# Attention with mixture of depths on one core: first loads ahead of a branch, mixture layers spread evenly and begun earlier

## Chip, cores and metric

The kernel runs on one NeuronCore of a Trainium2 chip. The metric is device time in microseconds (us), the median of several runs. All arithmetic is in float32.

## The reference

There are 8 batches of 448 tokens and 12 heads of 64 dimensions. First comes attention with normalized queries and keys, then, for each batch, a gate picks 128 tokens that pass through a two-layer network:

```python
q_n, k_n = (rmsnorm(q, g_q), rmsnorm(k, g_k))
scores = scale * np.matmul(q_n, k_n.transpose(0, 1, 3, 2))
scores = scores - np.max(scores, axis=-1, keepdims=True)
attn = np.exp(scores)
attn = attn / (np.sum(attn, axis=-1, keepdims=True) + 1e-09)
x = np.matmul(attn, v)                      # then (B, H, S, D) -> (B, S, H*D)
scores = np.einsum('bsd,d->bs', x, w_gate)
for b in range(B):
    top_idx = np.argpartition(-scores[b], capacity)[:capacity]   # capacity = 128
    xe = x[b, top_idx]
    ye = np.maximum(xe @ w1, 0.0) @ w2                           # 768 -> 1024 -> 768
    g = 1.0 / (1.0 + np.exp(-scores[b, top_idx]))
    out[b, top_idx] = x[b, top_idx] + g[:, None] * ye
```

## The kernel before

**Branch.** The program first loads g_q and g_k on the queue of SP, bounds the scores from them on VectorE (the bound test, lines 1193 to 1198) and every engine branches on the outcome (L1205, L1207). The inputs take the branch `fast`; `general` is not executed.

**Groups and units.** Four heads make a group: three groups to a batch, 24 in all. Each group has seven units of 64 keys, 168 units in all. A unit is `scores` (PE, L278), the exponential of its scores on ScalarE (L287), `values` (PE, L304, accumulated over the seven units of a group) and the running sum of the exponentials on VectorE (L317). Ahead of that, a group's queries and keys are squared (ScalarE, L193), summed (VectorE, L199) and turned into reciprocal roots (GpSimd, L200 and L203). For groups 2 to 23 these go through memory (`rows_out`, `rows_in`) and scale the queries (`scale_q`); for groups 0 and 1 `scale_q_early` does it with matmuls (L249) and VectorE (L257).

**Start of `fast`.** SP issues the loads of groups 0 and 1 (L102) in the order tok(0,0), tok(0,1), q(0), tok(1,0), k(0), tok(1,1), v(0), q(1), k(1), v(1). ScalarE's queue loads the gain column gcol (L133) and loads its table with a first exponential (L139). VectorE makes `gg` from gcol (L145); this stands ahead of the first sum of squares in its program. PE runs 60 transposes of an identity (L151) before its first useful matmul.

**After a group.** `values_out` copies the two accumulators to xT. Then four tasks follow, one at a time: `sum_keys` (L339, copied at L350), `invert_sums` (L357, L359), and `to_tokens` for the two halves (L371, scaled on VectorE at L373). After the second half come `gate` (L397) and, for the third group of a batch, `store_x` (SP, L385) and `spread` (VectorE, L413). `ranks_of` is queued as the next task: `score_rows` (PE, L426, ScalarE L430), `count` (VectorE, L440), `annotate` (L459), `select` (four scatters on GpSimd into the memory tile `selected`, L467), and `load_selected` (SP, L485), which brings the selected tokens back as `xe`.

**The mixture layer of a batch** is a generator of ten pieces: two of transposes of `xe` (L505, copied by ScalarE at L510), four of the first matrix (L524, two of them to an activation at L533), four of the second (L543, two of them to a combination at L552). The last piece issues the scatter to the output on GpSimd (L561). The two of transposes are light on PE, the eight others (*heavy*) take some 2.7 us each.

**Order.** Everything is emitted by hand in program order, section by section; each engine runs its own part in that order. A section `q` has four units: first `scores` of its units with `values` behind them, then one task (`opening`), then two halves. In each half the work that was set for its slots is issued (`run`), then a mixture piece (`piece`), then one task. A slot is a unit's number, so section `q` holds slots 4q to 4q + 3. After section 41 the units are used up and the loop runs on until the layers are done. `ready[b]` is the first section in which the layer of batch b may begin:

```python
ready[b] = max((s + 4) // PER + 1, first_ff(b) - 1) if b < B - 1 else 0
```

Here `s` is the slot at which `ranks_of` ran, and `first_ff` is a lower bound that grows by 21 units with each batch. Once begun, a layer gives one piece to each half until it is done.

Of the kernel before, what the change touches and what calls it, by code (L numbers as in the profile page):

```python
# [23 lines left out]


@with_exitstack
def fast(
    ctx: ExitStack,
    tc: tile.TileContext,
    qT: bass.AP,  # L30
    kT: bass.AP,
    vp: bass.AP,
    tok: bass.AP,
    g2: bass.AP,
# [19 lines left out]

    B, NP, _, S = qT.shape
    CP = 112
# [16 lines left out]
    const = ctx.enter_context(tc.tile_pool(name="const", bufs=1))  # L73
    load_pool = ctx.enter_context(tc.tile_pool(name="load", bufs=2))
    norm_pool = ctx.enter_context(tc.tile_pool(name="norm", bufs=2))
# [21 lines left out]

    toks, qTs, kTs, vs, sss, rinvs, bcs = {}, {}, {}, {}, {}, {}, {}

    def load(name, store, src, shape, n, bufs):  # L100
        t = load_pool.tile(shape, F32, name=name, bufs=bufs)
        nc.sync.dma_start(out=t, in_=src)  # L102
        store[n] = t

    def load_tok(n, i):
        load("tok", toks, tok[n // NG, n % NG, :, i], [128, 2, NI, D], (n, i), 4)

    def load_q(n):
        c = n % NG * 2
        load("qT", qTs, qT[n // NG, c : c + 2].rearrange("c p s -> p c s"), [128, 2, S], n, 3)  # L110

    def load_k(n):
        c = n % NG * 2
        load("kT", kTs, kT[n // NG, c : c + 2].rearrange("c p s -> p c s"), [128, 2, S], n, 3)

    def load_v(n):
        load("v", vs, vp[n // NG, n % NG], [128, 2, NI, D], n, 3)

    ident = const.tile([128, 128], F32, name="ident")
    make_identity(nc, ident)  # L120
    load_tok(0, 0)
    load_tok(0, 1)
    load_q(0)
    load_tok(1, 0)
    load_k(0)
    load_tok(1, 1)
    load_v(0)
    load_q(1)
    load_k(1)
    load_v(1)  # L130

    gcol = const.tile([128, 2], F32, name="gcol")
    nc.scalar.dma_start(out=gcol, in_=g2)  # L133
    gg = const.tile([128, 1], F32, name="gg")
    neg_half = const.tile([128, 1], F32, name="neg_half")
    nc.vector.memset(neg_half, -0.5)

    warm = const.tile([128, 1], F32, name="warm")
    nc.scalar.activation(out=warm, in_=neg_half, func=AF.Exp)  # L139

# [8 lines left out]
    ps = ps_moe.tile([128, 512], F32, tag="moe", name="warm_ps")  # L149
    for _ in range(60):  # L150
        nc.tensor.transpose(out=ps[:, 0:128], in_=ident, identity=ident)  # L151
# [38 lines left out]
    def squares(n, i):  # L190
        t = toks.pop((n, i))
        sq = norm_pool.tile([128, 2, NI, D], F32, name="sq")
        nc.scalar.activation(out=sq, in_=t, func=AF.Square, scale=scale)  # L193
        sss[n, i] = norm_pool.tile([128, 2, NI], F32, name="ss", bufs=4)
        return sq
# [38 lines left out]
    def scale_q(n):  # L234

        t = qTs[n]
        nc.vector.scalar_tensor_tensor(
            out=t, in0=t, scalar=gg, in1=bcs.pop(n), op0=OP.mult, op1=OP.mult
        )

    def scale_q_early(n):

        rinv = rinvs.pop((n, 0))
        for c in range(2):
            ps = ps_sc.tile([128, 512], F32, tag="sc", name="sc")
            r = slice(D * c, D * (c + 1))
            for i in range(NI):
                for hh in range(2):
                    nc.tensor.matmul(  # L249
                        out=ps[D * hh : D * (hh + 1), D * i : D * (i + 1)],  # L250
                        lhsT=rinv[r, hh, i : i + 1].to_broadcast([D, D]),
                        rhs=ident[r, r],
                        start=True,
                        stop=True,
                    )
            t = qTs[n][:, c].rearrange("d (p i) -> d p i", i=NI)
            nc.vector.scalar_tensor_tensor(  # L257
                out=t,
                in0=t,
                scalar=gg,  # L260
                in1=ps[:, 0:S].rearrange("d (i p) -> d p i", i=NI),
                op0=OP.mult,
                op1=OP.mult,
            )
# [5 lines left out]
    def scores(u):  # L270
        n, i = divmod(u, NI)
        scs = [ps_sc.tile([128, 512], F32, tag="sc", name="sc") for _ in range(2)]
        for c in range(2):
            for k0 in (0, 32):
                for hh in range(2):
                    r = slice(D * hh, D * (hh + 1))
                    o = D * c + k0
                    nc.tensor.matmul(  # L278
                        out=scs[hh][o : o + 32, 0:S],
                        lhsT=kTs[n][r, c, D * i + k0 : D * i + k0 + 32],  # L280
                        rhs=qTs[n][r, c, :],
                        start=True,
                        stop=True,
                    )
        p = p_pool.tile([128, 2, S], F32, name="p")
        for hh in range(2):
            nc.scalar.activation(  # L287
                out=p[:, hh],
                in_=scs[hh][:, 0:S],
                func=AF.Exp,  # L290
                scale=rinvs[n, 1][:, hh, i : i + 1],
            )
        probs[u] = p

    def values(u):
# [3 lines left out]
        for hh in range(2):  # L299
            for d0 in (0, 32):  # L300
                for c in range(2):
# [3 lines left out]
                        out=avs[n][c][o : o + 32, 0:S],  # L305
                        lhsT=vs[n][r, hh, i, d0 : d0 + 32],
                        rhs=probs[u][r, hh],
# [266 lines left out]
    HALVES = 2  # L574
    PER = 2 * HALVES
    units = n_groups * NI
    todo, tasks = {}, []
# [25 lines left out]
    for n in range(1, n_groups):  # L603
        s0 = NI * n
        if n > 2:
            at(max(s0 - 26, 0), load_tok, n, 0)
            at(max(s0 - 26, 0), load_tok, n, 1)
        if n > 1:
            first = max(s0 - 18, 0)
            prepare(n, first)  # L610
            at(max(s0 - 7, first + 10), scale_q, n)
            at(max(s0 - 13, 2), load_q, n)
            at(max(s0 - 11, 2), load_k, n)
            at(max(s0 - 11, 2), load_v, n)
    for part in range(NDC + NFC):
# [21 lines left out]
    def last_tokens(n):  # L637
# [8 lines left out]
        q, place = now  # L646
        tasks.insert(0, ((q + 1, place // 2), lambda: ranks_of(b)))

    def ranks_of(b):
# [6 lines left out]
        at(s + 4 if s >= 0 else s + 3, load_selected, b)  # L656
        ready[b] = max((s + 4) // PER + 1, first_ff(b) - 1) if b < B - 1 else 0

    def first_ff(b):


        return -(-(units + 2 * PER - NG * NI * (B - 2 - b)) // PER)

# [20 lines left out]
    sum_squares(1, 1, sq.pop((1, 1)))  # L684
    load_tok(2, 0)
    load_tok(2, 1)
    tasks.append(((0, 1), lambda: scale_q_early(1)))
# [5 lines left out]

    def piece(q):

        nonlocal moe, done
        if next(moe, moe) is not moe:
            return True
        if ready.get(done, q + 1) > q:
            return False  # L700
        moe = mixture(done)
        done += 1
        next(moe)
        return True

    waiting = list(range(units))
    moe, ready, done, q = iter(()), {}, 0, 0
    while done < B or tasks:
        now[:] = q, 0
# [7 lines left out]
        for half in range(HALVES):  # L717
            run((k + 2 * half, k + 2 * half + 1))
            some = piece(q)
            spare[0] = not some and half == 0  # L720
# [4 lines left out]
        q += 1  # L725
    for _ in moe:
        pass


@with_exitstack  # L730
def general(
# [33 lines left out]
    load_pool = ctx.enter_context(tc.tile_pool(name="load", bufs=2))  # L765
    norm_pool = ctx.enter_context(tc.tile_pool(name="norm", bufs=2))
    tr_pool = ctx.enter_context(tc.tile_pool(name="tr", bufs=3))
# [12 lines left out]
    def load(n):  # L780

        b, h0 = n // NG, n % NG * GH
        for nm, src in (("q", q), ("k", k), ("v", v)):
            t = load_pool.tile(
                [CP, GH, NJ, D], F32, tag=nm, name=nm, bufs=5 if nm == "v" else 3
            )
# [186 lines left out]
    def mixture(b):  # L973
# [36 lines left out]
        for j in range(NJ):  # L1010
            cmp = moe_pool.tile([CP, S], F32, name="cmp", bufs=2)
            nc.vector.tensor_scalar(
# [7 lines left out]
            )  # L1020
            cmp = moe_pool.tile([CP, S], F32, name="cmp", bufs=2)
            nc.vector.scalar_tensor_tensor(
# [35 lines left out]
        for s in range(NSLOT):  # L1058
# [45 lines left out]
            for f0 in range(0, NFC, 4):  # L1104
                ps = bank()
                for i in range(4):
# [8 lines left out]
                    if i % 2:  # L1115
# [6 lines left out]
                        yield  # L1122
            y = moe_pool.tile([128, DM], F32, name="y", bufs=2)
            for half in range(2):
# [58 lines left out]
def _build(nc, ap, cap, out):  # L1183
    D = ap["g_q"].shape[0]
    with tile.TileContext(nc) as tc:
        with tc.tile_pool(name="bound", bufs=1) as pool:
            g = pool.tile([1, 2, D], F32, name="g")
            nc.sync.dma_start(out=g[:, 0], in_=ap["g_q"].rearrange("(one d) -> one d", one=1))
            nc.sync.dma_start(out=g[:, 1], in_=ap["g_k"].rearrange("(one d) -> one d", one=1))

# [16 lines left out]
        with tc.If(is_small > 0) as cmp, tc.manual_schedule():  # L1207
            fast(
                tc, *(ap[n] for n in ("qT", "kT", "vp", "tok", "g2")),
                *(ap[n] for n in _INS[5:]), cap, out,  # L1210
            )
# [45 lines left out]
```

## Time and profile before

| | |
|---|---|
| median of 3 runs | 550.41 us (549.37 to 550.66) |
| profiled execution | 546.3 us |
| its span, first to last instruction | 544.4 us |
| mean granted TensorE clock | 0.988 |
| busy: PE / VectorE / ScalarE / GpSimd | 515.7 / 347.3 / 279.4 / 215.3 us |
| L278 and L304, PE busy | 155.3 and 155.7 us |
| L524 and L543, PE busy | 69.2 and 61.2 us (in the loop's main part) |

The profile is of one execution. A row of the timeline gives the start, the time, the engine (PE is TensorE's matmuls, PEld its weight loads, DVE is VectorE, ACT is ScalarE, POOL is GpSimd, SPq, ACTq and POOLq are the queues' instructions that issue transfers), the line, the operation, what is written from what, and the count of merged instructions; in brackets stand the engine's idle time before it and what ended that. A row of the windows gives, for a stretch of time, its length, each engine's busy time with its count, the granted clock of TensorE, the busy share of the DMA engines and GB/s.

### The profile page before, as it was taken

The page shows a single profiled execution, that of the slowest core. Times are in us where ns is not written, and L with a number is a line of the kernel's source. Part 1 is how long each engine was busy: PE and PEld are TensorE (multiplying, and loading weights), DVE is VectorE, ACT ScalarE, POOL GpSimd, SP SyncE. Part 2 cuts the span into 40 slices and gives each one's busy share as a digit, 9 for nine tenths or more (in the row PEclk, how much of TensorE's full clock was granted, in tenths as well). Part 3 has the DMA queues.
Part 4 walks back from the last instruction along what each step waited for, and adds up shares of the span by engine and source line. Part 5 has one row for each costly group of instructions (what it writes and reads, how often), then busy time and mean ns, then how long its engine had stood idle before and what let it go on. Part 6 is the DMA issues. An engine that isn't in the chain of part 4 may idle for free. (4 is left out here: it accounts for less than half of the span.)

```text
span 544.4 us, 16414 instructions
## 1 busy us (share of the span) xinstructions
PE 515.7 (95%) x7084; PEld 293.2 (54%) x7084; DVE 347.3 (64%) x651; ACT 279.4 (51%) x506; POOL 215.3 (40%) x149
## 2 busy tenths in 40 slices
PE   6999989999999899999999999998999999989994
PEld 6544333346644476446744466443664466549682
DVE  3688999899575766659557795758657384463000
ACT  3788777785544755455455755455555444310100
POOL 3875887754542352425514453323614103002000
PEclk9999999999999999999999999998999999997998
DMA  6938999988645567538536477605652231004000
GB/s 223 364 128 259 302 338 301 290 302 277 222 143 187 167 192 215 137 124 253 182 135 183 155 233 229 188 24 170 226 138 67 101 104 59 2 29 131 30 31 34
DMA packets 46532, 93.55 MB, mean 172 GB/s; under 512 B 11382, under 2 KB 29302, under 8 KB 46452
## 3 DMA queue, kind: packets, MB, share of 16 engines
q1 hardware_dynamic: 43108, 86.12, 49.6%
q0 software_dynamic: 3200, 6.31, 3.3%
q8 instruction: 57, 0.93, 0.7%
q14 instruction: 23, 0.19, 0.1%
q10 hardware_dynamic: 144, 0.00, 0.0%
HBM read 74.93 MB, written 25.35 MB: 184 GB/s over the span
## 5 line engine op out<-in xcount | busy, mean ns | idle before, releaser
L287 ACT ACTIVATE p<-sc,rinv 128x448 f32<-128x448 f32 x336 | 186.6, 639 | 98.2 <-PE sc L278 75.5
L304 PE MATMUL av<-p,v 64*32 64x448 f32 x2688 | 155.7, 537 | 0.5 <-issue 0.5
L278 PE MATMUL sc<-qT,kT 64*32 64x448 f32 x2688 | 155.3, 542 | 0.2
L203 POOL TENSOR_TENSOR rinv<-ss,neg_half 128x14 f32<-128x14 f32 x48 | 136.9, 2852 | 4.0
L317 DVE TENSOR_TENSOR sum<-sum,p 128x896 f32<-128x896 f32 x120 | 130.5, 1088 | 11.3 <-ACT p L287 3.0
L304 PEld LDWEIGHTS av<-p,v 64*32 64x32 f32 x2688 | 58.6, 107 | 74.4 <-issue 66.6
L278 PEld LDWEIGHTS sc<-qT,kT 64*32 64x32 f32 x2688 | 50.4, 106 | 70.3 <-issue 51.1
L200 POOL TENSOR_SCALAR ss<-ss 128x14 f32<-128x14 f32 x48 | 23.1, 481 | 163.4 <-DVE ss L199 146.6
L524 PE MATMUL moe_ps<-xeT,w 128*128 128x128 f32 x576 | 69.2, 277 | 0.0
L524 PEld LDWEIGHTS moe_ps<-xeT,w 128*128 128x128 f32 x576 | 66.2, 192 | 4.3 <-issue 4.3
L373 DVE TENSOR_TENSOR x<-x_ps,rden 112x512 f32<-112x512 f32 x48 | 33.0, 689 | 50.9 <-PE x_ps L371 45.3
L199 DVE TENSOR_REDUCE ss<-sq 128x14 f32<-128x896 f32 x48 | 51.8, 1079 | 21.1 <-ACT sq L193 21.1
L543 PE MATMUL moe_ps<-w,hT 128*128 128x384 f32 x176 | 61.2, 491 | 0.0
L467 POOL DMA_INDIRECT selected<-x,rank x32 | 36.7, 1147 | 59.4 <-DVE x L459 43.5
L561 POOL DMA_INDIRECT out_dram<-xe,row x8 | 11.3, 1419 | 92.8 <-DVE rden L359 55.8
L193 ACT ACTIVATE sq<-tok 128x896 f32<-128x896 f32 x48 | 44.7, 959 | 5.4 <-DMA tok<-in_tok_dram 5.0
L543 PEld LDWEIGHTS moe_ps<-w,hT 128*128 128x128 f32 x176 | 31.7, 190 | 21.8 <-issue 2.9
L397 DVE SCALAR_TENSOR_TENSOR prod<-x,wg 112x256 f32<-112x256 f32 x96 | 41.1, 428 | 2.7
L552 DVE SCALAR_TENSOR_TENSOR xe<-sc,xe 128x384 f32<-128x384 f32 x5 | 3.1, 618 | 44.7 <-PE sc L543 44.7
L371 PEld LDWEIGHTS x_ps<-ident,xT 128*112 128x112 f32 x192 | 21.0, 134 | 19.1 <-issue 12.7
L350 ACT COPY den<-den_ps 128x224 f32<-128x224 f32 x24 | 8.3, 347 | 44.2 <-PE den_ps L339 44.0
L371 PE MATMUL x_ps<-ident,xT 128*112 128x128 f32 x192 | 29.1, 278 | 1.4 <-DVE x L373 1.4
(63 smaller groups left out, 340.8 us busy)
## 6 DMA issues: line engine op xcount, KB each, us to landing
tok<-in_tok_dram SPq DMA_DIRECT2D x48, 448.0 KB
qT<-in_qT_dram SPq DMA_DIRECT2D x24, 448.0 KB
kT<-in_kT_dram SPq DMA_DIRECT2D x24, 448.0 KB
v<-in_vp_dram SPq DMA_DIRECT2D x24, 448.0 KB
out_dram<-x SPq DMA_DIRECT2D x8, 1344.0 KB
bc<-rows SPq DMA_DIRECT2D x44, 224.0 KB
xe<-selected SPq DMA_DIRECT2D x8, 385.0 KB
w<-in_moe_w_dram SPq DMA_DIRECT2D x6, 512.0 KB
```

Of the source, the lines that this page charges most:

```text
L193: nc.scalar.activation(out=sq, in_=t, func=AF.Square, scale=scale)
L199: nc.vector.tensor_reduce(out=ss, in_=sq, axis=AX.X, op=OP.add)
L203: nc.gpsimd.tensor_tensor(out=rinv.rearrange(flat), in0=ss.rearrange(flat), in1=neg_half.to_broadcast([128, 2 * NI]), op=OP.pow,)
L278: nc.tensor.matmul(out=scs[hh][o : o + 32, 0:S], lhsT=kTs[n][r, c, D * i + k0 : D * i + k0 + 32], rhs=qTs[n][r, c, :], start=True, stop=True,)
L287: nc.scalar.activation(out=p[:, hh], in_=scs[hh][:, 0:S], func=AF.Exp, scale=rinvs[n, 1][:, hh, i : i + 1],)
L304: nc.tensor.matmul(out=avs[n][c][o : o + 32, 0:S], lhsT=vs[n][r, hh, i, d0 : d0 + 32], rhs=probs[u][r, hh], start=(i == 0), stop=(i == NI ...
L317: nc.vector.tensor_tensor(out=sums[n], in0=probs[u - 1] if i == 1 else sums[n], in1=probs[u], op=OP.add)
L371: nc.tensor.transpose(out=ps[:CP, j, :], in_=t[:, j, :], identity=ident)
L397: nc.vector.scalar_tensor_tensor(out=prod, in0=xs[b][:, j, cols], scalar=1.0, in1=wg[:, cols], op0=OP.mult, op1=OP.mult, accum_out=gates[b ...
L467: w = nc.gpsimd.indirect_dma_start(out=t[:, :], out_offset=bass.IndirectOffsetOnAxis(ap=rank[:, j : j + 1], axis=0), in_=x[:, j, :], in_of ...
L524: nc.tensor.matmul(out=ps[:, 128 * i : 128 * i + n], lhsT=w1[:, dc, 128 * (f0 + i) : 128 * (f0 + i + 1)], rhs=xeT[:, dc, :n], start=(dc == 0),
L543: nc.tensor.matmul(out=ps[:n, : DM // 2], lhsT=hT[:, fc, :n], rhs=w2[:, fc, cols], start=(fc == 0), stop=(fc == NFC - 1),)
```

## The change

- A class `Loads` is set up before the bound test. It fills `neg_half`, runs the first exponential, and issues tok(0,0), tok(0,1), q(0) and k(0) on SP. The loads of g_q and g_k for the test go to ScalarE's queue. The other first loads follow in `fast`: tok(1,0), tok(1,1), v(0), q(1), k(1), v(1). gcol is still loaded after the branch.
- PE runs 36 transposes at the start in place of 60.
- The layer of a batch begins at the section that `ready` gives with a lower bound of 9, 14, 20, 25, 30, 35, 41 for batches 0 to 6 in place of 12, 17, 22, 28, 33, 38, 43, and its ten pieces are paced over 21 units (ten and a half halves) for batches 0 to 5. The layers of batches 6 and 7 are not paced.
- The task `ranks_of` of the last batch comes after the first mixture piece of the next section (its first half) in place of the section's beginning.
- Some buffers of `general` are fewer; the buffers of `v` have a pool of their own.

```diff
+class Loads:
+    def __init__(self, nc, pool, qT, kT, vp, tok):
...
+        neg_half = pool.tile([128, 1], F32, name="neg_half", bufs=1)
+        nc.vector.memset(neg_half, -0.5)
+        warm = pool.tile([128, 1], F32, name="warm", bufs=1)
+        nc.scalar.activation(out=warm, in_=neg_half, func=AF.Exp)
+        self.neg_half = neg_half
+        self.load("tok", 0, 0)
+        self.load("tok", 0, 1)
+        self.load("qT", 0)
+        self.load("kT", 0)
...
-    load_tok(0, 0)
-    load_tok(0, 1)
-    load_q(0)
-    load_tok(1, 0)
-    load_k(0)
-    load_tok(1, 1)
-    load_v(0)
-    load_q(1)
-    load_k(1)
-    load_v(1)
+    load("tok", 1, 0)
+    load("tok", 1, 1)
+    load("v", 0)
+    for name in ("qT", "kT", "v"):
+        load(name, 1)
...
-    for _ in range(60):
+    for _ in range(36):
         nc.tensor.transpose(out=ps[:, 0:128], in_=ident, identity=ident)
...
+    PIECES = 2 + 2 * (NFC // 4) + 4
...
         q, place = now
-        tasks.insert(0, ((q + 1, place // 2), lambda: ranks_of(b)))
+        later = place // 2 if b < B - 1 else 1
+        tasks.insert(0, ((q + 1, later), lambda: ranks_of(b)))
...
-        ready[b] = max((s + 4) // PER + 1, first_ff(b) - 1) if b < B - 1 else 0
+        ready[b] = max((s + 4) // PER + 1, first_ff(b)) if b < B - 1 else 0
 
     def first_ff(b):
-        return -(-(units + 2 * PER - NG * NI * (B - 2 - b)) // PER)
+        return (units - PER - NG * NI * (B - 2 - b)) // PER
...
-    def piece(q):
-        nonlocal moe, done
-        if next(moe, moe) is not moe:
-            return True
-        if ready.get(done, q + 1) > q:
-            return False
-        moe = mixture(done)
-        done += 1
+    def piece(q, half):
+        nonlocal moe, done, pieces
+        if pieces == PIECES:
+            if ready.get(done, q + 1) > q:
+                return False
+            moe = mixture(done)
+            done += 1
+            pieces = 0
+        elif done < B - 1:
+            passed = HALVES * (q - ready[done - 1]) + half
+            if passed * PIECES * PER < pieces * HALVES * NG * NI:
+                return False
         next(moe)
+        pieces += 1
         return True
...
-            nc.sync.dma_start(out=g[:, 0], in_=ap["g_q"].rearrange("(one d) -> one d", one=1))
-            nc.sync.dma_start(out=g[:, 1], in_=ap["g_k"].rearrange("(one d) -> one d", one=1))
+            nc.scalar.dma_start(out=g[:, 0], in_=ap["g_q"].rearrange("(one d) -> one d", one=1))
+            nc.scalar.dma_start(out=g[:, 1], in_=ap["g_k"].rearrange("(one d) -> one d", one=1))
+            loads = Loads(nc, load_pool, *(ap[n] for n in ("qT", "kT", "vp", "tok")))
```

## The prediction

> **What bounds the kernel now.** I read the page's busy shares and its 40 slices first.
>
> ```profile
> PE 515.7 (95%) x7084; PEld 293.2 (54%) x7084; DVE 347.3 (64%) x651; ACT 279.4 (51%) x506; POOL 215.3 (40%) x149
> ...
> PE   6999989999999899999999999998999999989994
> ...
> DVE  3688999899575766659557795758657384463000
> ...
> PEclk9999999999999999999999999998999999997998
> ```
>
> TensorE is busy nearly everywhere, and its work is the same after the change, so only its gaps can move. They lie at the head, in slices 3 to 10, where VectorE is at 8 or 9 tenths, and at the end. I cut PE's timeline at the first L278 of every section. Sections with two heavy mixture pieces (L524, L543) take 12 to 14 us, those of attention alone 7 to 10 us. Taking off each section's matmuls at their unobstructed spacing (0.047 us for each L278 or L304, 0.112 for L524, 0.323 for L543) leaves 9.5 us of gaps in sections 0 to 8 and 32 us in 9 to 40. About 0.9 us goes with every change of group (L339, L357 and the switch of av banks).
>
> The head, from the timeline of all engines:
>
> ```profile
> 4.03 0.83 SPq L102 DMA_DIRECT2D tok<-in_tok_dram  x2
> 4.31 0.40 ACTq L133 DMA_DIRECT2D gcol<-in_g_dram  x1
> ...
> 7.65 0.95 ACT L193 ACTIVATE sq<-tok 128x896 f32<-128x896 f32 x1 [1.36 <-DMA tok<-in_tok_dram]
> ...
> 7.84 0.16 DVE L145 SCALAR_TENSOR_TENSOR gg<-gcol 128x1 f32<-128x1 f32 x1 [3.04 <-DMA gcol<-in_g_dram]
> ...
> 8.63 1.09 DVE L199 TENSOR_REDUCE ss<-sq 128x14 f32<-128x896 f32 x1 [0.63 <-ACT sq L193]
> ```
>
> See that tok needs 3.6 us from issue to use, and that on VectorE gg stands ahead of the first sum of squares and waits for gcol until 7.84.
>
> PE at a section that holds only the two transposes of a layer (17), from its timeline:
>
> ```profile
> 180.86 0.65 PE L371 MATMUL x_ps<-ident,xT 128*112 128x128 f32 x4 [0.46 <-DVE x L373]
> 181.75 0.55 PE L505 MATMUL moe_ps<-ident,xe 128*128 128x128 f32 x3 [0.24 <-ACT xeT L510]
> 183.17 0.58 PE L339 MATMUL den_ps<-sum,pick_pair 128*32 128x224 f32 x8 [0.87 <-DVE x L373]
> ```
>
> With no heavy piece PE outruns the others and waits three times. The longest such waits, and the clock by windows:
>
> ```profile
> 373.74 0.90 PE L426 MATMUL row_ps<-ident,spread 112*112 112x112 f32 x4 [2.60 <-DVE spread L413]
> ```
>
> ```profile
> 490.60 0.96 PE L426 MATMUL row_ps<-ident,spread 112*112 112x112 f32 x4 [3.11 <-DVE parts L418]
> ```
>
> ```profile
> 374.00:377.50 3.50, 3.50 (x35) 1.54 (x41) 2.15 (x7) 1.46 (x4) 0.00 (x0) 0.53 0.97 316
> ...
> 491.00:497.00 6.00, 6.00 (x32) 6.00 (x31) 3.43 (x13) 0.64 (x2) 0.91 (x1) 0.52 0.69 232
> ```
>
> The column before the last two is the granted clock: it fell to half just after each of these waits, for 3.4 and 6.8 us by the trace's clock record, costing 1.7 and some 3 us.
>
> **What the Trainium skill says.** "TensorE: Matmul & The Clock Gate", Part 1: an idle window of about 3.4 us drops the array to half clock, a busy window lifts it. This trace agrees in kind; waits of 2.6 and 3.1 us between transposes sufficed. "DMA: Bandwidth & Descriptors", Queues, rings and completion order: queues of different engines share the DMA engines, which alternate by packet. gcol agrees: issued at 4.31 on ACT's queue between the tok loads, it landed at 7.8. The same page, Anatomy of one DMA, gives a software DMA some 2 us beyond its data: the last scatter of selected ended on POOL at 500.75 and SP went on at 502.66, 1.9 us; in the busy stretch at 90.27 it took until 95.5.
>
> **Part by part.**
>
> *Head.* Four loads go out at about 0.8 instead of 4.03, so tok is usable at 0.8 + 3.6 = 4.4. The branch must still be passed (3.9), then ACT issues gcol (0.40): the first L193 at about 4.75 instead of 7.65, 2.9 earlier. But L145 still waits for a gcol issued after the branch, again among large packets. With gcol as late as now, L199 starts at 8.0 instead of 8.63. I take 0.7 earlier; the ends are 0 (g, moved from SP to ACT's queue, now meets tok packets and delays the test) and 1.7 (gcol lands within 2.5 us). Second: the 60 warm transposes end at 13.57 while rinv was ready at 12.78; 24 fewer at 0.109 are 2.6 us, so warming ends near 11, before rinv. That gives back the rest of 0.7. On ACT, issuing g and the table load (1.28) fit before 3.4. SP's other loads keep their order except that kT passes tok of group 1; they start no later. Sum **-1.3** (0 to -2.6).
>
> *Layer of batch 0 at section 9.* ready[0] becomes max(32/4 + 1, 9) = 9, so the first L505 stands in the first half of section 9, ahead of L339. Its input, from the timeline:
>
> ```profile
> 91.55 2.92 PE L304 MATMUL av<-p,v 64*32 64x448 f32 x48
> ...
> 95.21 0.59 PE L339 MATMUL den_ps<-sum,pick_pair 128*32 128x224 f32 x8 [0.74 <-DVE sum L317]
> ...
> 95.52 0.33 SPq L485 DMA_DIRECT2D xe<-selected  x1
> ```
>
> L485 waits for the scatters (POOL, 83.8 to 90.3); its semaphore is complete at 99.9. Today nobody wants it until 117.6. After, PE reaches L505 at 94.45 and waits 5.4 us, with every later matmul queued behind it; 0.7 of that replaces the wait of L339, so 4.7. VectorE catches up meanwhile, which saves some 0.4 in section 10. Such a wait should halve the clock for a window: +1.7 (0 to 3.4). Sum **+6.0** (4.0 to 8.0).
>
> *Layers 1 to 6.* Worked through the loop, the first L505 of layers 1 to 5 moves to sections 14, 20, 25, 30, 35 and of layer 6 to 41 (today 17, 22, 28, 33, 38, 43), ten pieces on ten and a half halves, so that the two transposes stand in different sections beside heavy pieces. Their xe: from annotate (L459) to landing took 9 to 13 us, and the tightest, layers 1 and 5, have about 2 us in hand. Today sections 12, 17, 22, 28, 33, 38 last 57.6 us for 45.7 us of work; of the 11.9, 4.7 is change of group (five at 0.94) and 0.6 half clock, leaving 6.6. Afterwards ten such halves keep perhaps 0.3 each, 3.0: -3.6. The 2.60 wait at 373.74 goes, since row_ps of batch 5 now follows a heavy piece, and its half clock, -1.7. Sum **-5.3** (-9 to -2). Earlier L561 on POOL and store_x behind it on SP: nothing on PE waits there today, 0 (-0.5 to +0.5).
>
> *The end.* With batch 6 four pieces further when its values end, the row_ps of batch 7 comes after L524, L524 and the first L543 piece: the 3.11 wait goes. But from row_ps (490.60) to xe landed (506.0) is 15.4 us of VectorE, POOL and two DMAs. Today eight pieces cover it:
>
> ```profile
> 502.66 0.33 SPq L485 DMA_DIRECT2D xe<-selected  x1
> ...
> 515.00 0.82 PE L505 MATMUL sc<-ident,xe 128*128 128x128 f32 x6
> ```
>
> After, only 0.6 for row_ps and three L543 pieces of 8 x 0.323 = 2.6 are left, 8.4 us: PE idles 7.0. Net +3.9. Half clock then falls on batch 7 instead of batch 6: -0.6 (-3 to +1). Sum **+3.3** (0.5 to 5).
>
> *Nothing:* buffers of the general branch (not executed), the pool of v, get() in place of pop(): no instruction of the path.
>
> **Sum:** -1.3 + 6.0 - 5.3 + 3.3 = **+2.7 us**. The profiled execution took 546.3 us (span 544.4 and 1.9 around it), which gives 549.0; the runs' median is 4.1 above it, so I forecast **553.1 us**. What a measurement here can tell from no change is about 0.3%, 1.7 us.
>
> **Rivals.**
> 1. *The even spread wins* (faster; 0.21). The gaps with change of group in sections 10 to 40 are VectorE being late, and a heavy piece in nearly every half hides them too. Sections 15, 20, 25 and 36, without such a change, have under 0.1 us of gaps. If 18 groups lose 0.45 of 0.9, 8 us go: 545. It outweighs the two new waits once over 4.4 us go this way. For it: VectorE at 8 to 9 tenths in slices 3 to 10. Against it: in 14, 16, 21 and 37 two heavy pieces are there and the gap stays.
> 2. *The waits come but are cheap* (same; 0.16). No half clock, or VectorE catching up, takes 2 us off: 551.
> 3. *More transposes wait for their selection* (slower; 0.12). Layers 1 and 5 miss by 1 to 2 us each and the clock halves: about +4, 557.
> 4. *No change at all* is excluded by the moved pieces.
>
> The forecast itself has 0.51; its own range is 550.5 to 555.5, whose lower edge gives 0.03 to "same". Faster 0.21, same 0.19, slower 0.60. The range 546.5 to 557.5 takes in most of rivals 1 and 3.
>
> **What would show it.** PE's L505 in section 9 waits some 5 us for DMA xe, the last layer's some 7; the clock falls to half behind each; L145 still waits for gcol; L249 starts near 12.2; no wait over 1 us remains ahead of row_ps from batch 1 on. The forecast is wrong if xe of batch 0 is there when PE comes, if the last idle is under 4 us, or if the gaps of sections 10 to 40 shrink by over 9 us.

## The result and the profile after

The changed kernel takes **578.83 us** (median of 4 runs, 577.54 to 579.74). The kernel before, on the same chip, takes 550.53. The ratio is 1.0507, with a 95% interval of 1.0467 to 1.0548. The forecast was 553.1: slower was right, but the loss is 28 us and not 2.7. Ratios here and below, with the 95% interval in brackets, leave out executions over 1.5% above the fastest of their kernel, so they can differ a little from the quotient of the medians beside them.

The page of the kernel after, busy shares and slices:

```profile
PE 521.5 (90%) x7060; PEld 288.7 (50%) x7060; DVE 348.4 (60%) x651; ACT 279.0 (48%) x506; POOL 215.1 (37%) x149
...
PE   4898999399899999999999999999899999999594
...
DVE  2466999374756566585765765665767636564100
...
PEclk9898999799999999999999999999999999999898
```

PE's busy time rose by 5.8 us only, though its share fell from 95 to 90%: the span grew by idle time. Two holes can be seen, a 3 in the eighth slice and a 5 near the end. These are the two waits that the forecast named. They do not add up to 28 us.

I cut PE's timeline by sections as the prediction did: the gaps are what remains of a section after its matmuls at their unobstructed spacing. In us:

| | first scores (L278, L284) at | sections 0-3 | 4-8 | 9-13 | 14-40 | 41 on |
|---|---|---|---|---|---|---|
| before | 15.3 | 4.9 | 4.6 | 5.7 | 26.0 | 7.0 |
| after | 17.8 | 12.0 | 4.6 | 18.8 | 33.4 | 10.1 |
| difference | +2.5 | +7.1 | 0 | +13.1 | +7.4 | +3.1 |

The differences sum to 33.2; the spans of the two profiled executions differ by 33.6. This is more than the 28.3 of the medians because the profiled execution of before lay 4.2 under its median and that of after 0.9 above.

**The head.** The timeline of the kernel after; L1208 is the bound test's first step, L144 and L151 answer to L133 and L145 of before, L255 to L249:

```profile
4.51 0.21 DVE L1208 TENSOR_TENSOR prod<-g 1x64 f32<-1x64 f32 x1 [3.59 <-DMA g<-in_g_k_dram]
...
6.33 0.39 ACTq L144 DMA_DIRECT2D gcol<-in_g_dram  x1
...
11.70 0.16 DVE L151 SCALAR_TENSOR_TENSOR gg<-gcol 128x1 f32<-128x1 f32 x1 [4.91 <-DMA gcol<-in_g_dram]
...
15.97 1.67 PE L255 MATMUL sc<-ident,rinv 64*64 64x64 f32 x56 [2.61 <-POOL rinv L209]
```

g lands 2 us later than before (L1193 started at 2.49), so the branch and gcol's issue come 2.0 later. gcol then takes until 11.7, where it was there at 7.84. VectorE's first sum of squares stands behind it. PE, with 36 warm transposes, runs dry for 2.61 us, and the clock record shows half clock from 18.3 to 21.7 behind it.

**Sections 0 to 3.** Here a cost appears that the forecast held at nothing. The waits of SP's queue, first of the kernel after and then of the kernel before (total us, times, longest; L56 and L102 issue the loads of tok, qT, kT and v):

```profile
SPq L56 <- PE sc L284: 197.0, 19, 17.8
...
SPq L56 <- ACT sq L199: 36.0, 17, 7.6
```

```profile
SPq L102 <- PE sc L278: 5.9, 11, 0.8
SPq L102 <- ACT sq L193: 4.5, 6, 1.6
```

SP waits 233 us in place of 10 until the readers of qT, kT and tok have let a buffer go. `bufs` still says 4 and 3. But the four tiles that `Loads` takes before the branch do not come back into use inside it. The trace shows this by what the loads wait for. In the kernel after, the load of a tok tile follows the squares (L199) of the tile two before it, and the load of a group's qT the last scores of the group two before it: two places each are in use. In the kernel before, the tok load follows the squares of the tile four before it, and qT is loaded while the scores of the group two before it still run. SP issues in program order, so the moves of the reciprocal roots through memory (`rows_out`, `rows_in`) stand behind the blocked loads. Before and after, the bc of group 2 and what waits for it:

```profile
31.54 1.25 SPq L228 DMA_DIRECT2D bc<-rows  x2
...
36.00 1.15 DVE L237 SCALAR_TENSOR_TENSOR qT<-qT,gg,bc 128x896 f32<-128x896 f32 x1 [0.45 <-DMA bc<-rows]
```

```profile
43.26 1.25 SPq L234 DMA_DIRECT2D bc<-rows  x2
...
47.83 1.15 DVE L243 SCALAR_TENSOR_TENSOR qT<-qT,gg,bc 128x896 f32<-128x896 f32 x1 [7.09 <-DMA bc<-rows]
...
49.08 3.24 PE L284 MATMUL sc<-qT,kT 64*32 64x448 f32 x32 [2.37 <-issue]
```

The queries of group 2 are scaled 11.8 us later, and the scores that need them start 1.25 us after that. "issue" names no cause here; the neighbouring L243 does. PE also runs these scores at half clock, which lasts from 49.0 to 52.4.

**The mixture layers.** PE's waits at the mixture's bank and transposes, after and then before:

```profile
PE moe_ps L511 <- DMA xe<-selected: 8.7, 1, 8.7
...
PE sc L511 <- DMA xe<-selected: 6.4, 1, 6.4
...
PE moe_ps L549 <- DVE xe L558: 3.3, 5, 1.3
...
PE moe_ps L530 <- ACT xeT L516: 1.9, 3, 1.1
PE moe_ps L530 <- ACT hT L539: 1.3, 6, 0.2
```

```profile
PE sc L524 <- ACT xeT L510: 0.3, 1, 0.3
PE moe_ps L505 <- ACT xeT L510: 0.2, 1, 0.2
```

The first two of after are the waits for the selected tokens of batches 0 and 7. The others were hardly there before. PE writes its sums into banks of the memory PSUM; up to section 41 the mixture has a single one, which two pieces of a matrix fill. At the start of the next filling PE waits here until ScalarE (L516, L539) or VectorE (L558) has emptied it. The windows around the wait of batch 0 (columns as in the prediction):

```profile
104.00:107.00 3.00, 0.15 (x7) 0.00 (x0) 3.00 (x3) 0.00 (x0) 1.96 (x1) 1.00 1.00 386
107.00:112.80 5.80, 0.00 (x0) 0.00 (x0) 1.15 (x2) 0.00 (x0) 0.00 (x0) 0.50 0.72 277
```

PE stands still, and the clock goes to half for 10.2 us by its record. The DMA engines are full up to 107, and xe takes 7.2 us from its issue (105.68) to use.

### The profile page after: what moved, and what is told of

Read it like the earlier page. It is cut to its first block, busy times and chain, and to the rows that moved or that the text cites. A ratio compares the mean times of both kernels' runs of the same rounds, so it can differ in the third digit from the quotient of the medians.

```text
span 578.0 us, 16350 instructions
## 1 busy us (share of the span) xinstructions
PE 521.5 (90%) x7060; PEld 288.7 (50%) x7060; DVE 348.4 (60%) x651; ACT 279.0 (48%) x506; POOL 215.1 (37%) x149
## 4 chain that ended last, share of the span: by engine, by line
PE 54%; issue 21%; DVE 9%; DMA 8%; ACT 3%; POOL 3%; SPq 0%; DVEq 0%; ACTq 0%; POOLq 0%
PE sc L284 16%; PE av L310 15%; PE moe_ps L530 9%; PE moe_ps L549 9%; DVE sum L323 3%; DMA xe<-selected 2%; DMA bc<-rows 2%; PE x_ps L377 2%; DMA selected<-x,rank 2%; POOL selected L473 1%; DVE ss L205 1%; POOL rinv L209 1%; DMA gcol<-in_g_dram 1%; PE den_ps L345 1%; DVE cmp L446 1%
## 5 line engine op out<-in xcount | busy, mean ns | idle before, releaser
L284 PE MATMUL sc<-qT,kT 64*32 64x448 f32 x2688 | 157.2, 552 | 3.2 <-issue 2.4
L284 PEld LDWEIGHTS sc<-qT,kT 64*32 64x32 f32 x2688 | 50.0, 108 | 75.5 <-issue 52.9
L206 POOL TENSOR_SCALAR ss<-ss 128x14 f32<-128x14 f32 x48 | 26.8, 559 | 162.6 <-DVE ss L205 122.0
L473 POOL DMA_INDIRECT selected<-x,rank x32 | 35.4, 1107 | 120.6 <-DVE x L465 109.4
L549 PE MATMUL moe_ps<-w,hT 128*128 128x384 f32 x192 | 67.3, 493 | 4.4 <-DVE xe L558 3.3
L199 ACT ACTIVATE sq<-tok 128x896 f32<-128x896 f32 x48 | 45.0, 957 | 11.3 <-DVE ss L205 4.3
L549 PEld LDWEIGHTS moe_ps<-w,hT 128*128 128x128 f32 x192 | 34.5, 190 | 28.5 <-DVE xe L558 4.6
L243 DVE SCALAR_TENSOR_TENSOR qT<-qT,gg,bc 128x896 f32<-128x896 f32 x22 | 25.5, 1160 | 13.5 <-DMA bc<-rows 8.9
L567 POOL DMA_INDIRECT out_dram<-xe,row x8 | 9.1, 1137 | 63.5 <-DVE xe L558 62.9
L446 DVE SCALAR_TENSOR_TENSOR cmp<-score_rows,gate,earlier 112x448 f32<-112x448 f32 x32 | 21.9, 685 | 16.2 <-ACT score_rows L436 15.1
```

Source lines behind the costliest of these rows:

```text
L284: nc.tensor.matmul(out=scs[hh][o : o + 32, 0:S], lhsT=get("kT", n)[r, c, D * i + k0 : D * i + k0 + 32], rhs=get("qT", n)[r, c, :], start=True,
L473: w = nc.gpsimd.indirect_dma_start(out=t[:, :], out_offset=bass.IndirectOffsetOnAxis(ap=rank[:, j : j + 1], axis=0), in_=x[:, j, :], in_of ...
L549: nc.tensor.matmul(out=ps[:n, : DM // 2], lhsT=hT[:, fc, :n], rhs=w2[:, fc, cols], start=(fc == 0), stop=(fc == NFC - 1),)
```

## The experiments

The theory after this reading had three parts: the buffers lost before the branch, the late gcol, and the pacing, which puts two fillings of the bank into one section. The rivals were that the early start of the layers, the selection waits above all, or the early loads themselves carry the loss. The experiments ran on three other chips, where the kernel before took 542.18 us (e1 to e4), 541.02 (e5 to e8) and 550.99 (e9 to e12); each is compared with runs of it on its own chip. The times expected for e1 to e4 were reckoned from the 550 of the chip of the result.

### e1: fewer buffers in the kernel before

```diff
     def load(name, store, src, shape, n, bufs):
+        first = n in (0, (0, 0), (0, 1)) and name != "v"
+        if name != "v":
+            bufs = bufs - 2 if name == "tok" else bufs - 1
+        if first:
+            name, bufs = name + "_first", 2 if name == "tok" else 1
```

The first four tiles get memory of their own, the others 2, 2 and 2 buffers.

> The kernel before, with the buffers that the changed program really rotates: tok(0,0), tok(0,1), q(0), k(0) keep memory of their own, and all later tok tiles share 2 buffers in place of 4, q and k 2 in place of 3. Theory A (the four tiles made before the branch are never given back inside it, and SP's queue then waits for buffers): 15 to 20 us slower than before, about 567. Theory B (the mixture's new schedule costs the time: selected tokens come too late): under 2 us, about 552. Theory C (the head): no change.

Measured: 548.6 against 542.18, ratio 1.0129 [1.0060, 1.0197]. SP waits as in the kernel after:

```profile
SPq L107 <- PE sc L283: 166.8, 19, 16.1
```

Sections 0 to 3 last 36.2 us against 30.9 in both traces of the kernel before. So the loss of buffers alone costs time, some 7 us, but in this order of loads less than half of what I expected.

### e2: the schedule alone

The kernel before with the changed `ready`, `first_ff`, `piece`, pacing and `later`; its head and buffers stay.

> The kernel before with the new schedule of layers alone (ready from 9, 14, 20, pacing, last ranks_of behind a piece); loads, buffers and start as before. Theory A: what the prediction summed for these parts, +4 us, up to +8 with the half clock behind longer waits: 554 to 558. Theory B: 20 us or more slower, 570 or above. Theory C: no change.

Measured: 558.05 against 542.18, ratio 1.0304 [1.0246, 1.0363], 16.5 us. Theory A had expected 4 to 8 us, so the schedule is no small part. e6 takes this apart.

### e3: the head alone

The changed kernel with `ready`, `first_ff`, `piece` and the place of `ranks_of` as before.

> The changed kernel with the schedule of layers of before: early loads, 36 warm transposes, and with them the lost buffers. Theory A: 2.5 us at the head and 15 to 20 for the buffers, about 570. Theory B: about 555. Theory C (the head alone loses all): 575 or more, with the loss before section 4.

Measured: 554.41 against 542.18, ratio 1.0217 [1.0152, 1.0281], 11.8 us. First scores at 18.4, gaps of sections 0 to 3 at 12.9. The head with its lost buffers is not the larger part: theory A had 570. The two parts add up: 3.04% and 2.17% are 5.2%, and the change cost 5.07%.

### e4: the changed kernel with fixed tiles used in turn

```diff
...
-        t = pool.tile(list(src.shape), F32, name=name, bufs=3 if i is None else 4)
+        ring = self.rings.setdefault(name, [])
+        k = n if i is None else 2 * n + i
+        size = 3 if i is None else 4
+        if k < size:
...
+            ring.append(pool.tile(list(src.shape), F32, name=f"{name}{k}", bufs=1))
+        t = ring[k % size]
```

> The changed kernel, with loads rotating over the same 4 (tok), 3 (q), 3 (k) tiles by hand, so that the tiles made before the branch are used again; no other edit. Theory A: most of the loss goes, 556 to 561. Theory B: 575 or more. Theory C: 575 or more.

Measured: 560.07 against 542.18, ratio 1.0331 [1.0274, 1.0388]. With four, three and three tiles the gaps of sections 0 to 3 are 4.9 again, as before the change, though first scores still come at 17.0. What is left is the schedule's 3.04% of e2, and hardly more. SP's wait for the readers of qT and kT is as short as before:

```profile
SPq L61 <- PE sc L289: 2.9, 6, 1.0
```

The time lies in theory A's 556 to 561 only because this chip is faster: of the 5.07% about a third went, not most.

### e5: the kernel before, looked at on the second chip

> The kernel before, unchanged, for a profile on the chip of these runs: the same PE order, so the waits of 2.6 us (row_ps of batch 5) and 3.1 us (row_ps of batch 7) must return; whether the half clock follows them is open. Span some 8 us shorter if the half clock is absent, 544 if not.

Measured: one profile, 540.67 us, span 538.8. The two waits returned. No half clock followed the one of 2.60 us, and one of 3.4 us that of 3.11. Sections 14 to 40 have 20.2 us of gaps where the chip of the result had 26.0; this trace is the base for e6 and e7, and for e2, whose chip had the same median for the kernel before (542.2 and 541.0).

### e6: early layers without pacing

e2 with `piece` and the loop as before: a layer still begins at sections 9, 14, 20 and so on, and the last scores still stand behind a piece, but a begun layer gives a piece to every half.

> The schedule-only kernel (early start, last ranks_of behind a piece) without the pacing: a layer's ten pieces follow each other as before, so that both pieces of a bank lie in one section. Theory D (the pacing shifts the bank's change into the middle of a section, where PE waits for ScalarE or VectorE to empty it, about 11 us in all): those waits go to under 1 us, the waits beside the two transposes come back (+5), in sum 5 to 8 us faster than schedule-only, about 8 to 10 us over before. Rival E (the early start itself costs, by the waits for xe of batches 0 and 7 and the half clock behind them): within 2 us of schedule-only, 14 to 17 us over before.

Measured: 544.38 against 541.02, ratio 1.0067 [1.0039, 1.0094], 3.6 us. So the pacing costs 2.4%, 12.8 us (3.5 either way by the two intervals). The gaps, with e5 as the base (e2 ran on another chip):

| | sections 4-8 | 9-13 | 14-40 | 41 on |
|---|---|---|---|---|
| e5, before | 4.6 | 6.5 | 20.2 | 5.7 |
| e6, early | 5.2 | 10.8 | 15.1 | 9.7 |
| e2, early and paced | 6.9 | 11.2 | 26.1 | 9.8 |

Most of the 11.0 us between e6 and e2 in sections 14 to 40 arise where the bank changes hands. Unpaced, the two pieces of one filling lie in one section, and the bank is first wanted again in the next section, behind four units of attention. Paced, a layer's halves hold T, nothing, T, F, F, F, F, S, S, S, S (T transposes, F first, S second matrix), so the pairs in one section are T F, F F, F S, S S, each from two fillings. Between them stands one task. In e2's timeline, PE (L524 pieces):

```profile
121.76 2.84 PE L524 MATMUL moe_ps<-xeT,w 128*128 128x128 f32 x24
124.44 0.60 PE L371 MATMUL x_ps<-ident,xT 128*112 128x128 f32 x4
125.29 2.94 PE L524 MATMUL moe_ps<-xeT,w 128*128 128x128 f32 x24 [0.25 <-ACT hT L533]
```

and in e6's, in the same place of a layer:

```profile
124.11 2.84 PE L524 MATMUL moe_ps<-xeT,w 128*128 128x128 f32 x24
126.79 0.60 PE L371 MATMUL x_ps<-ident,xT 128*112 128x128 f32 x4
127.23 2.84 PE L524 MATMUL moe_ps<-xeT,w 128*128 128x128 f32 x24
```

The pieces start 3.53 us apart in the one and 3.12 in the other. Ahead of the first matmul of the 20 fillings for L524 and L543 of layers 1 to 5, the starts lie 10.4 us in all beyond the unobstructed spacing in e2 and 2.0 in e6. In e2 6.8 us of this are waits that the trace names, in e6 none. One gap of 1.4 stands where four L440 of `count` are ahead of L552 on VectorE and the last ends 0.8 us after the filling. PE's waits in e2:

```profile
PE moe_ps L543 <- DVE xe L552: 3.6, 6, 1.3
...
PE moe_ps L524 <- ACT xeT L510: 1.8, 3, 1.1
PE moe_ps L524 <- ACT hT L533: 1.3, 6, 0.3
```

Of the 8.4 us between 10.4 and 2.0, 2.9 stand ahead of the first L524 and the first L543 of a layer. These read xeT and hT, which the copy or activation that empties the bank writes, so a second bank would not spare them. The other 5.5 are the bank alone. No run gave the layer a second one. In e6 the list has no line for L524 or L543. It has the waits for xe:

```profile
PE moe_ps L505 <- DMA xe<-selected: 6.9, 2, 6.4
PE sc L505 <- DMA xe<-selected: 6.8, 1, 6.8
```

Theory D had +8 to +10 us for e6, with +5 for the waits beside the two transposes. These did not come back: the gaps of the sections that hold both transposes are about 3.5 us (14, 20, 25, 30, 35) where e5 has about 10 (17, 22, 28, 33, 38).

### e7: only the last scores behind a piece

```diff
-        tasks.insert(0, ((q + 1, place // 2), lambda: ranks_of(b)))
+        later = place // 2 if b < B - 1 else 1
+        tasks.insert(0, ((q + 1, later), lambda: ranks_of(b)))
```

> The kernel before with one edit: ranks_of of the last batch after the first mixture piece of its section. Eight pieces of batch 6 are left there, so xe of batch 7 still comes in time. Theory D and the prediction's step: the 3.1 us wait ahead of row_ps goes and nothing takes its place: 3 us faster than before, up to 6 if a half clock goes with it. Rival: the selection is later by the piece and PE waits at the end: no change.

Measured: 536.46 against 541.02, ratio 0.9929 [0.9902, 0.9956]. This part of the change pays by itself. The row_ps of batch 7 in the timeline:

```profile
484.53 0.59 PE L426 MATMUL row_ps<-ident,spread 112*112 112x112 f32 x4 [0.17 <-DVE spread L413]
...
503.34 0.82 PE L505 MATMUL sc<-ident,xe 128*128 128x128 f32 x6
```

The wait of 3.11 us is 0.17, no half clock follows, and seven pieces still cover the selection: L505 does not wait.

### e8: the head put right

The kernel before with the four early loads and fixed tiles as in e4; g stays first on SP, gcol is issued on ScalarE's queue ahead of the branch, and 30 warm transposes remain.

> The kernel before with early loads done so that nothing is lost by them: g_q and g_k first on SP's queue and tok, q, k behind them, gcol on ScalarE's queue before the branch too, the tiles used again by hand, 30 warm transposes. Theory F (the head of the changed kernel loses because g and gcol share the DMA engines with the large loads): the test is done at about 3.4 as before, gg no longer waits, first scores at 12 to 12.5 in place of 15.3, 3 us faster than before. Rival: what follows the head is bound by GpSimd and the loads of groups 2 and 3, and the gain is gone by section 4: no change.

Measured: 537.33 against 541.02, ratio 0.9958 [0.9932, 0.9984]. In the timeline gg (L157 here) no longer waits:

```profile
0.78 0.37 ACTq L31 DMA_DIRECT2D gcol<-in_g_dram  x1
...
4.95 0.21 DVE L157 SCALAR_TENSOR_TENSOR gg<-gcol 128x1 f32<-128x1 f32 x1
```

First scores come at 13.0, 2.8 us earlier than in e5.

### e10 and e11: which part of the head was late

e10 is e8's schedule and tiles with the changed kernel's order: g on ScalarE's queue, gcol after the branch, 36 transposes. e11 differs in two lines:

```diff
-            nc.scalar.dma_start(out=g[:, 0], ...)
-            nc.scalar.dma_start(out=g[:, 1], ...)
+            nc.sync.dma_start(out=g[:, 0], ...)
+            nc.sync.dma_start(out=g[:, 1], ...)
```

> The changed kernel's head (four loads ahead of the test, g on ACT's queue, gcol after the branch, 36 warm transposes) with the schedule of before, and with tok, qT and kT in 4, 3 and 3 fixed tiles used in turn, so that no buffer is lost. Theory A (of the 12 us that this head cost with its lost buffers, the buffers are about 10): only the later first scores remain, as 17.0 us against 15.3: +1 to +2 us over before, ratio 1.002 to 1.004, gaps of sections 0 to 3 at 5 us. Theory B (the early loads themselves crowd the head): +6 us or more, ratio over 1.010.

> The same as e10 with one difference: the two loads of g stand first on SP's queue, as before the change, with the four loads behind them; gcol is still issued after the branch. Theory A (g on ACT's queue beside the four loads delayed the test by 2.0 us, and gcol with it): prod starts near 2.5 us instead of 4.5, gcol is issued 2 us earlier, and first scores come at about 15 instead of 17: 2 us faster than e10, level with before. Theory B (gcol is late because it is issued among large packets, whenever that is): gg still starts near 11 us, first scores at about 16.5, no more than 0.5 us faster than e10.

Measured: e10 551.3 against 550.99, ratio 1.0005 [0.9980, 1.0031]; e11 552.44, ratio 1.0036 [1.0010, 1.0061]. With its buffers kept, the changed head costs nothing that can be told. So the lost buffers are the difference between e3 and e10: 2.1%, about 11.5 us. The changed kernel against e4, which differ in nothing else, gives 1.7%, about 9.5 us. Each pair ran on two chips, and the intervals leave 4 us either way. In e11 the test and the branch are early again, and yet:

```profile
4.34 0.40 ACTq L149 DMA_DIRECT2D gcol<-in_g_dram  x1
...
11.14 0.16 DVE L156 SCALAR_TENSOR_TENSOR gg<-gcol 128x1 f32<-128x1 f32 x1 [6.35 <-DMA gcol<-in_g_dram]
```

Theory B: gg starts at 11.14 with gcol issued at 4.34, and at 10.93 with gcol issued at 6.01 (e10), so g's queue does not matter. Moving g back was no gain; moving gcol ahead of the loads was (e8, which also has six warm transposes fewer, 0.65 us).

### e9 and e12: the two gains together, and the changed kernel again

e9 is e8 with e7's edit. e12 is the changed kernel.

> The kernel before with the two parts that paid when done alone: the mended head (-3.7 us) and the scores of the last batch behind its first piece (-4.6 us). Theory A: the two lie at opposite ends of the span and share nothing, so they add: -8.3 us, ratio 0.985 (533 us where before takes 541). Theory B: a start 2.7 us earlier shifts the work of the last batch against its mixture, and part of either is lost: ratio 0.989 or above.

> The changed kernel as it is, on the chip of e9 to e11, so that its parts are sized beside it. Theory A (schedule +16, buffers about +10, head +2, and they add): 569 us where before takes 541, ratio 1.052. Theory B (the parts overlap on this chip, since PE lacks here the issue stalls of the first chip): ratio 1.040 or less.

Measured: e9 541.77 against 550.99, ratio 0.9827 [0.9787, 0.9867], faster than both kernels, by 1.7% and by 6.4% (541.77 against 579.05). That is more than 0.71% and 0.42% of e7 and e8 together; their intervals leave it open whether anything beyond a sum is there. e12 579.05, ratio 1.0503 [1.0446, 1.0561]: the loss is the same on this chip as on that of the result.

## Why the prediction was wrong in size

That "slower" came true is in part luck. The forecast of +2.7 was a balance of four terms, and the loss comes from two costs that the sum did not hold: it had the buffers at nothing and the pacing as a gain. By the experiments the loss is made of 9.5 to 11.5 us for the buffers, 12.8 for the pacing, 3.6 for the early layers and hardly anything for the rest of the head.

**Buffers: "Nothing" became about 11.5 us (e3 less e10; 9.5 by the changed kernel less e4).** This is one of the two large failures. I asked whether the moved lines add instructions, and did not ask where tiles live. The `get()` in place of `pop()` and `v`'s pool were indeed nothing, but the four tiles taken outside the branch were lost to the branch. e1 shows that the loss alone costs time, e4 and e10 that giving it back takes the cost away. Why e1 costs less than e3 I have not settled; the intervals (0.6 to 2.0% and 1.5 to 2.8%) overlap, and the order of the first loads differs.

**Layers 1 to 6: "-5.3" became +5.9 (e2 less e5, sections 14 to 40).** The failed step is "Afterwards ten such halves keep perhaps 0.3 each": I counted the waits of the transposes that would go, and did not follow who empties the single bank between two halves. e6, without pacing, has -5.1 there, but that this fits -5.3 is in part luck: I had argued that the two transposes would stand apart beside heavy pieces, and in e6 they stand in one section as before. Its gain lies in where these sections fall; no `score_rows` (L426) stands in one of them, where before those of batches 4 and 5 did. No run tells more. The 2.60 us wait for row_ps of batch 5 did go in e6 (0.21) and e2 (none); in the kernel after, two waits there of 1.97 and 1.72 us came, for batches 1 and 5 (e4, with its buffers, has none), against my "no wait over 1 us". The pacing, which I took to be the gain, costs 12.8 us: two fillings of the one bank, or a piece and its operand, stand one task apart.

**Head: "-1.3" became +2.5 at the first scores.** "With gcol as late as now" failed: gcol was later, 11.7 for 7.84, because the loads issued early were under way when it was issued. I had asked only from when it is issued, not what is ahead of it. In time this hardly counted (e10).

**Batch 0: "+6.0" was right in kind.** The wait of 5.4 us is 3.8 in e2, 6.4 in e6 and 8.7 in the kernel after; the half clock follows in all three. Sections 9 to 13 lose 4.3 us more in e6 than in e5. In the kernel after they lose 13.1 more: loads of tok, kT, v and a weight are issued in the 6 us ahead of xe, whose transfer takes 7.2 us instead of 3.5 in e2. I put this down to the buffers' loss once more; e4 has a wait of 4.8.

**The end: "+3.3" was right.** It measured +3.1 after the change and +4.0 in e6. The idle of "7.0" was 6.4 to 6.9, with 6.8 us of half clock behind it.

The sum of my three schedule terms, +4.0, is what e6 measured (3.6, interval 2.1 to 5.1): the number fits the schedule without its pacing, which is not the one that I reckoned. Rival 1, that an even spread wins, is refuted. Rival 3 did not happen: layers 1 to 5 wait for a selection once, for 0.5 us in e6, and not at all in e2 or the kernel after.

"TensorE: Matmul & The Clock Gate", Part 1, of the Trainium skill gives an idle window of about 3.4 us for the drop to half clock. The waits for xe of 3.8 to 8.7 us fit that, but it is no safe threshold: see below.

## What to carry to other kernels

When a tile's allocation moves outside a branch or a loop, count the buffers that are left inside, and look at the waits of the queue that issues its loads; in a queue that issues in order, one missing buffer makes everything behind it late. Before spreading the pieces of a layer evenly, ask which pieces share an accumulator bank or feed each other, and keep the change where other matmuls cover the emptying. Issue small operands that everything waits for ahead of the large loads, and test the parts of a change one by one: one part of this change pays as it stands (e7), the early loads pay once gcol goes ahead of them (e8; both in e9, ratio 0.983), and two parts cost 22 to 24 us.

## What was unexpected of the hardware

- A small load's time depends on what is in flight when it is issued. gcol took from 4.31 to 7.84 behind two tok loads before the change, from 4.34 to 11.14 with four large loads issued before 3.3 and six more around it (e11). The time is not fixed for one program either: in the kernel after it was 5.4 us (6.33 to 11.70), in e12, the same kernel, 3.8 (6.34 to 10.11). The DMA engines were at 0.97 of their time from 3 to 11 us in the kernel after.
- The half clock does not follow a wait of a given length each time. In the kernel before, the wait of 2.60 us for row_ps of batch 5 was followed by it on the chip of the result, and the same wait at 372.39 in e5 was not. The 6.8 us behind the wait of batch 7 before the change began at 489.9, which is 0.7 before the wait ended and not after it, as the prediction has it. Shorter waits can bring it too. In e2 waits of 1.67 and 0.49 us ahead of L339 and L357 were followed by half clock from 80.6, the same two ahead of 77.75 and 78.83 in the kernel before were not. In e5 half clock came at 183.7 behind waits of 0.46, 0.37 and 0.87 us, which the kernel before has too (0.46, 0.24 and 0.87), without it.
- Single sections of the same kernel hold 1 to 2 us more of gaps on one chip than on another, for example sections 14, 24 and 40 before the change, inside runs of L304 where the profile shows nothing that PE waited for, and not in e5 (26.0 against 20.2 us of gaps in sections 14 to 40). No run here shows the cause.
